# Attention backward: three one-bank buffers for the dP product, transposes in three steps, column fills of X spread singly

## The chip, the cores and the metric

The kernel runs on one core of a Trainium2 chip. The metric is the device time of one execution in microseconds (us), and the median of several executions is quoted. "PE" is the matmul engine, "PEld" its weight loads, DVE, ACT and POOL are the vector, scalar and GpSimd engines, SP issues the DMAs. A PSUM "bank" is one of eight pieces of the matmul's output memory (the Trainium skill, "PSUM — Partial Sum Buffer", Specifications (TRN2): 8 banks of 2 KiB per partition). All eight are in use in this kernel, before and after, so a bank given to one tile is taken from another.

## The reference

Forward and backward pass of an E-Branchformer block: two sequences of 4000 tokens, 144 channels, bf16. Only attention matters here:

```python
scores = jnp.einsum('btd,bsd->bts', q, k) * D ** (-0.5)
p = _softmax(scores, axis=-1)
attn = jnp.einsum('bts,bsd->btd', p, v)
# ... and the gradients of all inputs by jax.vjp with grad_out
```

The kernel folds the weights so that, for a block of 128 query rows, S = Q·xaᵀ gives the scores, dP = B·xaᵀ the gradient of the probabilities, P = exp(S), Sm = dP*P, and then y needs the transposes of P and Sm (by DMA), and the "column fills" X = Smᵀ·Qs + Pᵀ·Bt are added into an accumulator in SBUF.

## The kernel before

There are 32 rows (blocks of 128 queries) per sequence, and four units (1000 key columns each) per row. The program fixes PE's order; the other engines' orders come from the compiler's scheduler.

```python
ps_s = tile_pool(name="at_pss", bufs=1, space=PSUM)   # S: one tile of 2 banks
ps_d = tile_pool(name="at_psd", bufs=1, space=PSUM)   # dP: one tile of 2 banks
ps_x = tile_pool(name="at_psx", bufs=2, space=PSUM)   # X: 2 tiles of 1 bank
ps_y = tile_pool(name="at_psy", bufs=1, space=PSUM)   # y: 1 bank
ps_j = tile_pool(name="at_psj", bufs=1, space=PSUM)   # transposes: 1 bank

def unit(i, c2):                     # (cut)
    pS = ps_s.tile([128, 2, 512], F32, tag="S")
    pD = ps_d.tile([128, 2, 512], F32, tag="D")
    for r, (p_, h) in enumerate(((pS, 0), (pD, 0), (pS, 1), (pD, 1))):   # the four "remainder" products (16 channels)
        nc.tensor.matmul(p_[:, h, 0:SC], QBr[rr, bi, :], S.XR[rr, c2, 0:SC], start=True, stop=False)
    for p_, w_ in ((pS, QTm), (pD, BTm)):                                # 128 channels, S then dP
        for h in range(2):
            nc.tensor.matmul(p_[:, h, 0:SC], w_[:, bi, :], S.xaT[:, c0:c0 + SC], start=False, stop=True)
    nc.scalar.activation(pd, pS[:, :, 0:SC], ACT.Exp, accum_out=...)      # P
    for h in range(2):
        nc.vector.scalar_tensor_tensor(Sm[...], pD[:, h, 0:SC], 1.0, P[...], op0=ALU.mult, op1=ALU.mult, accum_out=...)

def xfill(pr, f):                    # (cut) 12 matmuls; pr: a pair of rows, f: one of 11 column groups
    X = ps_x.tile([128, 3, D], F32, tag="x")
    ...
    if f % 3 == 2:                   # emptied by ACT, added by POOL
        nc.scalar.copy(xs[:, 0:nj, :], X[:, 0:nj, :])
        nc.gpsimd.tensor_tensor(a_, xs[:, 0:nj, :], a_, op=ALU.add)
    else:                            # added by DVE straight from X
        nc.vector.tensor_tensor(a_, X[:, 0:nj, :], a_, op=ALU.add)

nfill = [1, 1, 2, 1, 1, 2, 1, 2]     # fills in the 8 units of two rows
for i in range(NBK + 2):             # (cut)
    for c2 in range(4):
        unit(i, c2)
        yz(i - 2, c2)                # 16 matmuls of y for the row before last
        if c2 == 3: row_end(i)       # l, rl, dd, nd, nr, Qs, br, Bt; starts the two DMA transposes
        if i % 4 == 2 and c2 == 1: jit(i // 4 + 1)    # 12 transposes of Q and B for the next four rows, 3 copies by DVE
        # then this unit's nfill[...] fills
```

## Time and profile before

| | before |
|---|---|
| time, median of 3 | 1789.49 us (1781.45 to 1790.64) |
| attention stretches, first to last exp | 472.8 and 470.8 us |
| four rows in the middle (median) | 58.8 us |
| of four rows, dP waiting for Sm | 3.65 us |
| of four rows, transposes waiting for their copies | 2.03 us |

How to read it. The windows view gives the busy time of each engine in a stretch. This is one from the middle of the first attention stretch (columns as its header says):

```profile
core 0: us, PE busy (x) PEld busy (x) DVE busy (x) ACT busy (x) POOL busy (x), PEclk, DMA share, GB/s
300.00:650.00 350.00, 338.16 (x3874) 245.40 (x3871) 205.93 (x657) 137.44 (x272) 60.87 (x104) 1.00 0.82 145
```

PE is busy 97% of it at full clock and no other engine comes near. But the Trainium skill warns of that number ("Perfetto Trace Analysis", Identifying the Most-Contended Engine): matmul occupancy does not measure the distance to the roof, because matmuls are pipelined. What helps is the distance between the starts of one matmul and the next. In the timeline y and X matmuls start every 0.062 us although each is listed with 0.23 us. All waits in this text are such distances, less the usual one.

The transposes, in the view of waits (engine, line, waited for whom, total us, times, longest):

```profile
engine line waited for: us in total, times, longest us
...
PE pj L1635 <- DVE QTm L1636: 6.0, 5, 1.2
...
PE pj L1635 <- DVE BTm L1636: 2.6, 5, 0.5
```

That is 300 us of the trace (350 to 650 us). The three groups of four transposes share one bank, so the second and the third wait until DVE has copied the one before. (The view leaves out what overlaps with the modelled tail of a matmul; by start distances it is 2.0 us per group of four rows.)

### The profile page before, as it was taken

Reading aid. Unit: us, or ns where it says so; the run is one execution under the profiler, and the core shown is the slowest. Engines: PE = TensorE matmul, PEld = TensorE weight load, DVE = VectorE, ACT = ScalarE, POOL = GpSimd, SP = SyncE. Lnnn points to the kernel's source line nnn. Section 1 sums busy time; section 2 is a strip of 40 time slices with the busy share of each in tenths; the row PEclk is TensorE's granted clock in tenths of the full one; section 3 lists DMA queues with packets and bytes.
Section 4 is the critical chain, followed back from the end, with each engine's and each line's share of the span. In section 5 each row is a group of like instructions: output and inputs, shape, how many; then the busy total and the mean of one; then the engine's idle time right before and its main releaser. Section 6 shows DMA issues by size and latency. Waiting matters only on the chain.

```text
span 1788.5 us, 38445 instructions
## 1 busy us (share of the span) xinstructions
PE 1398.8 (78%) x15110; PEld 1035.2 (58%) x15110; DVE 1042.9 (58%) x3693; ACT 577.9 (32%) x1275; POOL 486.0 (27%) x831
## 2 busy tenths in 40 slices
PE   6666338999999999976566644899999999986663
PEld 3455315676667667866445431567766776776641
DVE  5778954665566555312877894555565655521393
ACT  3444213343334334211244421334333333411020
POOL 2666411111111111102766641111111111110160
PEclk9777557999999999998788855899999999999775
DMA  3111216787879788544411121788877887854320
GB/s 90 47 60 35 60 31 119 142 154 135 143 142 153 143 143 153 134 122 107 122 54 60 34 61 39 132 142 150 139 143 141 154 143 139 156 116 122 97 61 10
DMA packets 614882, 193.44 MB, mean 108 GB/s; under 512 B 584132, under 2 KB 610436, under 8 KB 614692
## 3 DMA queue, kind: packets, MB, share of 16 engines
q1 hardware_dynamic: 613828, 190.81, 54.2%
q8 instruction: 120, 1.97, 0.4%
q14 instruction: 70, 0.57, 0.1%
q10 hardware_dynamic: 864, 0.09, 0.0%
HBM read 37.48 MB, written 12.06 MB: 28 GB/s over the span
## 4 chain that ended last, share of the span: by engine, by line
PE 52%; DVE 22%; issue 8%; POOL 7%; SPq 4%; ACT 3%; DMA 3%; POOLq 0%; DVEq 0%; ACTq 0%
PE y L1692 11%; PE pS L1654 8%; PE X L1711 6%; PE X L1710 6%; DVE Sm L1660 5%; PE pD L1654 5%; PE pS L1650 4%; SPq L1348 4%; PE pD L1650 3%; ACT Pm L1657 2%; POOL gn_t L1515 2%; DVE goT L1590 1%; PE po L1790 1%; POOL rstd_g L1511 1%; PE EF L1776 1%
## 5 line engine op out<-in xcount | busy, mean ns | idle before, releaser
L1660 DVE SCALAR_TENSOR_TENSOR Sm<-pD,Pm 128x500 bf16<-128x500 f32 x512 | 326.8, 675 | 349.0 <-ACT Pm L1657 349.0
L1657 ACT ACTIVATE Pm<-pS 128x1000 bf16<-128x1000 f32 x256 | 256.9, 1003 | 516.7 <-PE pS L1654 516.7
L1711 PE MATMUL X<-Bt,Pm 128*128 128x144 bf16 x2048 | 282.1, 226 | 0.5 <-DVE Bt L1680 0.5
L1710 PE MATMUL X<-Qs,Sm 128*128 128x144 bf16 x2048 | 282.2, 226 | 0.0
L1710 PEld LDWEIGHTS <-Sm 128*128 128x128 bf16 x2048 | 200.4, 98 | 0.8 <-issue 0.8
L1711 PEld LDWEIGHTS <-Pm 128*128 128x128 bf16 x2048 | 200.4, 98 | 0.0
L1650 PE MATMUL pS<-XR,QBr 16*128 16x500 bf16 x512 | 162.0, 395 | 7.0 <-ACT Pm L1657 6.0
L1654 PE MATMUL pS<-xaT,QTm 128*128 128x500 bf16 x512 | 161.6, 399 | 0.0
L1654 PE MATMUL pD<-xaT,BTm 128*128 128x500 bf16 x512 | 159.2, 394 | 0.0
L1692 PEld LDWEIGHTS <-ST 128*128 128x128 bf16 x2048 | 138.9, 99 | 28.5 <-issue 1.6
L1692 PEld LDWEIGHTS <-PT 128*128 128x128 bf16 x2048 | 138.0, 98 | 29.3 <-issue 2.2
L1692 PE MATMUL y<-xaa,ST 128*128 128x144 bf16 x2048 | 151.0, 228 | 0.0
L1692 PE MATMUL y<-xaa,PT 128*128 128x144 bf16 x2048 | 149.9, 227 | 0.7 <-DVE B_t L1700 0.5
L1716 POOL TENSOR_TENSOR acc_3148<-xs,acc_3148 128x432 f32<-128x432 f32 x48 | 52.9, 1102 | 240.6 <-ACT xs L1715 240.6
L1716 POOL TENSOR_TENSOR acc_15091<-xs,acc_15091 128x432 f32<-128x432 f32 x48 | 52.9, 1101 | 238.9 <-ACT xs L1715 238.9
L1650 PE MATMUL pD<-XR,QBr 16*128 16x500 bf16 x512 | 103.4, 391 | 16.2 <-DVE Sm L1660 12.0
L1650 PEld LDWEIGHTS <-QBr 16*128 16x128 bf16 x1024 | 40.6, 91 | 110.8 <-issue 81.4
L1677 POOL TENSOR_SCALAR Qs<-Q_t,rl 128x144 bf16<-128x144 bf16 x64 | 24.6, 384 | 256.8 <-DVE rl L1669 207.5
L1715 ACT COPY xs<-X 128x432 f32<-128x432 f32 x96 | 49.7, 518 | 132.2 <-PE X L1711 132.2
L1654 PEld LDWEIGHTS <-BTm 128*128 128x128 bf16 x512 | 52.2, 102 | 65.0 <-issue 11.1
L1718 DVE TENSOR_TENSOR acc_3148<-X,acc_3148 128x432 f32<-128x432 f32 (+1 forms) x128 | 74.1, 582 | 20.4 <-PE X L1711 20.3
L1718 DVE TENSOR_TENSOR acc_15091<-X,acc_15091 128x432 f32<-128x432 f32 (+1 forms) x128 | 74.1, 582 | 18.8 <-PE X L1711 18.7
(1282 smaller groups left out, 2727.4 us busy)
## 6 DMA issues: line engine op xcount, KB each, us to landing
gs<-in_grad_out_dram SPq DMA_DIRECT2D x24, 720.0 KB, 5.2
gs<-in_grad_out_dram SPq DMA_DIRECT2D x8, 540.0 KB, 4.0
xg<-in_x_dram SPq DMA_DIRECT2D x28, 144.0 KB, 2.4
dh_d_491<-dh SPq DMA_DIRECT2D x8, 288.0 KB, 3.0
dh<-dh_d_491 SPq DMA_DIRECT2D x8, 288.0 KB
dh_d_12434<-dh SPq DMA_DIRECT2D x8, 288.0 KB, 2.3
dh<-dh_d_12434 SPq DMA_DIRECT2D x8, 288.0 KB, 3.0
out_dram<-og SPq DMA_DIRECT2D x14, 144.0 KB, 3.8
```

Of the source, the lines that this page charges most:

```text
L1348: nc.sync.dma_start(self.r[m * DR:(m + 1) * DR, g % self.ring, :], self.st[self.p0 + DR:self.p0 + 32, g * 512 + m:g * 512 + m + w])
L1515: nc.gpsimd.tensor_scalar(gn_t[g][:, hf * 2 + q, :], h_[:, q, D:2 * D], nm[:, q:q + 1], rstd_g[:, i0 + q:i0 + q + 1], op0=ALU.add, op1=ALU ...
L1650: nc.tensor.matmul(p_[:, h, 0:SC], QBr[rr, bi, :], S.XR[rr, c2, 0:SC], start=True, stop=False)
L1654: nc.tensor.matmul(p_[:, h, 0:SC], w_[:, bi, :], S.xaT[:, c0:c0 + SC], start=False, stop=True)
L1657: nc.scalar.activation(pd, pS[:, :, 0:SC], ACT.Exp, accum_out=st["l", i][:, c2:c2 + 1])
L1660: nc.vector.scalar_tensor_tensor(Sm[:, pb, c1:c1 + SC], pD[:, h, 0:SC], 1.0, P[:, pb, c1:c1 + SC], op0=ALU.mult, op1=ALU.mult, accum_out=s ...
L1692: nc.tensor.matmul(y[:, w, :], src[:, tb, j, :], S.xaa[:, j, :], start=(j == 0), stop=(j == NBK - 1))
L1710: nc.tensor.matmul(X[:, jj, :], Sm[:, pb, j * 128:(j + 1) * 128], Qs[:, pb, :], start=(kk == 0), stop=False)
L1711: nc.tensor.matmul(X[:, jj, :], P[:, pb, j * 128:(j + 1) * 128], Bt[:, pb, :], start=False, stop=(kk == 1))
L1715: nc.scalar.copy(xs[:, 0:nj, :], X[:, 0:nj, :])
L1716: nc.gpsimd.tensor_tensor(a_, xs[:, 0:nj, :], a_, op=ALU.add)
L1718: nc.vector.tensor_tensor(a_, X[:, 0:nj, :], a_, op=ALU.add)
```

## The change

The intent is to take both waits from PE. dP gets three one-bank buffers, so its bank is free earlier; X pays with one of its two banks. To live with one X bank, the eleven fills of a pair of rows no longer stand two in a row but before and after the y products ("places"). The transposes are done in three steps in three different units, their copies go to ACT, small operations move from DVE to POOL and ACT, and exp and Sm get a raised priority in the scheduler. The diff is whole:

```diff
--- before.py
+++ after.py
@@ -1604,8 +1604,8 @@
         sm = es.enter_context(tc.tile_pool(name="at_sm", bufs=4))
         xp = es.enter_context(tc.tile_pool(name="at_xs", bufs=2))
         ps_s = es.enter_context(tc.tile_pool(name="at_pss", bufs=1, space=PSUM))
-        ps_d = es.enter_context(tc.tile_pool(name="at_psd", bufs=1, space=PSUM))
-        ps_x = es.enter_context(tc.tile_pool(name="at_psx", bufs=2, space=PSUM))
+        ps_d = es.enter_context(tc.tile_pool(name="at_psd", bufs=3, space=PSUM))
+        ps_x = es.enter_context(tc.tile_pool(name="at_psx", bufs=1, space=PSUM))
         ps_y = es.enter_context(tc.tile_pool(name="at_psy", bufs=1, space=PSUM))
         ps_j = es.enter_context(tc.tile_pool(name="at_psj", bufs=1, space=PSUM))
         P = ab.tile([128, NP, GW], BF, name="Pm")
@@ -1622,19 +1622,17 @@
         jt = {}
         id_ = W.ident
 
-        def jit(g):
+        def jit(g, step):
             r = slice(g * 4, g * 4 + 4)
-            QTm = xp.tile([128, 4, 128], BF, tag="QTm")
-            BTm = xp.tile([128, 4, 128], BF, tag="BTm")
-            QBr = xp.tile([128, 4, 128], BF, tag="QBr")
-            for off, src in ((0, S.Q_t), (32, S.B_t), (64, S.Q_t), (96, S.B_t)):
-                nc.gpsimd.tensor_scalar(QB[:, :, off:off + DR], src[:, r, 128:D], 1.0, 0.0, op0=ALU.mult, op1=ALU.add)
-            for dst, src in ((QTm, S.Q_t[:, r, 0:128]), (BTm, S.B_t[:, r, 0:128]), (QBr, QB[:])):
-                pj = ps_j.tile([128, 4, 128], BF, tag="j")
-                for j in range(4):
-                    nc.tensor.transpose(pj[:, j, :], src[:, j, :], id_[:])
-                nc.vector.tensor_copy(dst[:], pj[:])
-            jt[g] = (QTm, BTm, QBr)
+            if step == 0:
+                jt[g] = [xp.tile([128, 4, 128], BF, tag=t_, name=t_) for t_ in ("QTm", "BTm", "QBr")]
+                for off, src in ((0, S.Q_t), (32, S.B_t), (64, S.Q_t), (96, S.B_t)):
+                    nc.gpsimd.tensor_scalar(QB[:, :, off:off + DR], src[:, r, 128:D], 1.0, 0.0, op0=ALU.mult, op1=ALU.add)
+            src = (S.Q_t[:, r, 0:128], S.B_t[:, r, 0:128], QB[:])[step]
+            pj = ps_j.tile([128, 4, 128], BF, tag="j")
+            for j in range(4):
+                nc.tensor.transpose(pj[:, j, :], src[:, j, :], id_[:])
+            nc.scalar.copy(jt[g][step][:], pj[:])
 
         def unit(i, c2):
             g, bi = divmod(i, 4)
@@ -1644,21 +1642,22 @@
                 st["l", i] = sm.tile([128, 4], F32, tag="l4", name="l4")
                 st["d", i] = sm.tile([128, 8], F32, tag="d8", name="d8")
             pS = ps_s.tile([128, 2, 512], F32, tag="S")
-            pD = ps_d.tile([128, 2, 512], F32, tag="D")
-            for r, (p_, h) in enumerate(((pS, 0), (pD, 0), (pS, 1), (pD, 1))):
+            pD = [ps_d.tile([128, 512], F32, tag="D", name="pD") for h in range(2)]
+            for r, o_ in enumerate((pS[:, 0, 0:SC], pD[0][:, 0:SC], pS[:, 1, 0:SC], pD[1][:, 0:SC])):
                 rr = slice(32 * r, 32 * r + DR)
-                nc.tensor.matmul(p_[:, h, 0:SC], QBr[rr, bi, :], S.XR[rr, c2, 0:SC], start=True, stop=False)
-            for p_, w_ in ((pS, QTm), (pD, BTm)):
+                nc.tensor.matmul(o_, QBr[rr, bi, :], S.XR[rr, c2, 0:SC], start=True, stop=False)
+            c0 = 2 * c2 * SC
+            for h in range(2):
+                nc.tensor.matmul(pS[:, h, 0:SC], QTm[:, bi, :], S.xaT[:, c0 + h * SC:c0 + (h + 1) * SC], start=False, stop=True)
+            for h in range(2):
+                nc.tensor.matmul(pD[h][:, 0:SC], BTm[:, bi, :], S.xaT[:, c0 + h * SC:c0 + (h + 1) * SC], start=False, stop=True)
+            with tc.high_priority():
+                pd = P[:, pb, c0:c0 + 2 * SC].rearrange("p (h c) -> p h c", h=2)
+                nc.scalar.activation(pd, pS[:, :, 0:SC], ACT.Exp, accum_out=st["l", i][:, c2:c2 + 1])
                 for h in range(2):
-                    c0 = (2 * c2 + h) * SC
-                    nc.tensor.matmul(p_[:, h, 0:SC], w_[:, bi, :], S.xaT[:, c0:c0 + SC], start=False, stop=True)
-            c0 = 2 * c2 * SC
-            pd = P[:, pb, c0:c0 + 2 * SC].rearrange("p (h c) -> p h c", h=2)
-            nc.scalar.activation(pd, pS[:, :, 0:SC], ACT.Exp, accum_out=st["l", i][:, c2:c2 + 1])
-            for h in range(2):
-                c1 = c0 + h * SC
-                nc.vector.scalar_tensor_tensor(Sm[:, pb, c1:c1 + SC], pD[:, h, 0:SC], 1.0, P[:, pb, c1:c1 + SC], op0=ALU.mult, op1=ALU.mult,
-                                               accum_out=st["d", i][:, 2 * c2 + h:2 * c2 + h + 1])
+                    c1 = c0 + h * SC
+                    nc.vector.scalar_tensor_tensor(Sm[:, pb, c1:c1 + SC], pD[h][:, 0:SC], 1.0, P[:, pb, c1:c1 + SC], op0=ALU.mult, op1=ALU.mult,
+                                                   accum_out=st["d", i][:, 2 * c2 + h:2 * c2 + h + 1])
 
         def row_end(i):
             pb = i % NP
@@ -1670,13 +1669,13 @@
             dd = sm.tile([128, 1], F32, tag="dd")
             nc.vector.reduce_sum(dd[:], d8[:], axis=AX.X)
             nd = sm.tile([128, 1], F32, tag="nd", bufs=6)
-            nc.vector.tensor_scalar(nd[:], dd[:], rl[:], -1.0, op0=ALU.mult, op1=ALU.mult)
+            nc.gpsimd.tensor_scalar(nd[:], dd[:], rl[:], -1.0, op0=ALU.mult, op1=ALU.mult)
             nr = sm.tile([128, 1], F32, tag="nr", bufs=6)
-            nc.vector.tensor_scalar(nr[:], nd[:], rl[:], None, op0=ALU.mult)
+            nc.gpsimd.tensor_scalar(nr[:], nd[:], rl[:], 1.0, op0=ALU.mult, op1=ALU.mult)
             st["rl", i], st["nr", i] = rl, nr
             nc.gpsimd.tensor_scalar(Qs[:, pb, :], S.Q_t[:, i, :], rl[:], 1.0, op0=ALU.mult, op1=ALU.mult)
             br = sm.tile([128, D], F32, tag="br")
-            nc.gpsimd.tensor_scalar(br[:], S.B_t[:, i, :], rl[:], 1.0, op0=ALU.mult, op1=ALU.mult)
+            nc.scalar.activation(br[:], S.B_t[:, i, :], ACT.Copy, scale=rl[:])
             nc.vector.scalar_tensor_tensor(Bt[:, pb, :], Qs[:, pb, :], nd[:], br[:], op0=ALU.mult, op1=ALU.add)
             tb = i % NT
             nc.sync.dma_start_transpose(out=PT[:, tb], in_=P[:, pb, :])
@@ -1717,25 +1716,28 @@
             else:
                 nc.vector.tensor_tensor(a_, X[:, 0:nj, :], a_, op=ALU.add)
 
-        nfill = [1, 1, 2, 1, 1, 2, 1, 2]
-        jit(0)
+
+        fills = {(0, 0): 0, (1, 0): 1, (1, 1): 2, (2, 0): 3, (3, 0): 4, (4, 0): 5, (4, 1): 6, (5, 0): 7, (6, 0): 8, (7, 0): 9, (7, 1): 10}
+        jsteps = {(1, 1): 0, (2, 1): 1, (3, 0): 2}
+        for step in range(3):
+            jit(0, step)
         with tc.manual_schedule(engines={mybir.EngineType.PE}):
             for i in range(NBK + 2):
+                pr, half = i // 2 - 1, i % 2
                 for c2 in range(4):
                     if i < NBK:
                         unit(i, c2)
-                    if 0 <= i - 2 < NBK:
-                        yz(i - 2, c2)
+                    for place in range(2):
+                        f = fills.get((half * 4 + c2, place))
+                        if f is not None and 0 <= pr < NBK // 2:
+                            xfill(pr, f)
+                        if place == 0 and 0 <= i - 2 < NBK:
+                            yz(i - 2, c2)
                     if c2 == 3 and i < NBK:
                         row_end(i)
-                    if i % 4 == 2 and c2 == 1 and i // 4 + 1 < NGR:
-                        jit(i // 4 + 1)
-                    pr = i // 2 - 1
-                    if 0 <= pr < NBK // 2:
-                        s = (i % 2) * 4 + c2
-                        f0 = sum(nfill[:s])
-                        for f in range(f0, f0 + nfill[s]):
-                            xfill(pr, f)
+                    g = i // 4 + 1
+                    if (i % 4, c2) in jsteps and g < NGR:
+                        jit(g, jsteps[i % 4, c2])
 
 
 def phase_merge_out(k, W, b, S):
```

## The prediction

> **What bounds the kernel.** By the windows table the two attention stretches (about 250-720 and 1095-1570 us) take 53% of the time and there PE is busy 48 of every 50 us at a granted clock of 1.00; DVE 29.5, ACT 20. So PE is nearly the limit there and only its stalls can be won. In the timeline the exps of one row of four units start 14.2, 14.0, 14.2 and 16.3 us after the last row's; the 16.3 is the row with the transposes.
>
> Start-to-start times of the matmuls in 350-700 us give one unit: four remainder products 0.31 us, S and dP 0.86, y 16 x 0.0625 = 1.0, fills 1.0 on average (128 matmuls in 8 units), changes 0.1: 3.28 us, 26.2 for two rows. Measured are 28.2 plus 1.05 for half of a transpose group. The missing 2.0 us is the second dP remainder waiting for the second Sm multiply of the unit before: 22.6 us in 96 units, 0.235 each. The loop is closed by latency: remainder to S 0.31, to exp 0.63, to first Sm 1.22, first Sm 0.6, second 0.68, release 0.06: 3.5 us. PE keeps matmul order (the Trainium skill, "PSUM — Partial Sum Buffer", Engine vs sequencer instructions); the trace agrees: S waits behind the blocked dP remainder.
>
> **What the change does.**
> 1. Three dP banks: that remainder waits for the first Sm, so the loop is 2.9 us, under PE's 3.28. Removes up to 2.0 us per two rows. In rows 0 and 1 (4.06 us per unit at the lower clock, 1.32 us of wait) about 0.67 per unit goes: 11 us in all.
> 2. Transposes: a group costs 2.1 us now, from waits for DVE copies (0.4 us each) on one bank. Twelve transposes at 0.055 are 0.66; spread, about 0.95 with changes. Saves 1.15 x 14 = 16 us.
> 3. X falls to one bank. A DVE add is 0.60 us, an ACT copy 0.52; between two fills of one unit lies 1.0 us of y. If DVE runs the add as soon as X is done, no stall. But X is done just as the exp is (both about 2.15 us after the unit's start), and the Sm multiplies have priority: behind them the add ends 1.9 us later and the second fill waits 1.0 us. Two of three double units use DVE: up to 2.1 us per two rows, 67 us over 32 pairs, cancelling step 1.
> 4. The first fill of a pair now precedes y, so Bt is needed 1.0 us sooner; Bt was ready just as the fill began (both 507.3 us). Up to 1.5 us per pair if adds go first. nd and nr on POOL and br on ACT shorten little.
>
> **Sum.** Step 1 at most 64 us, rows 0-1 11, step 2 16: 91 us, 1698. Steps 3 and 4 take back some 20 to 75 of it. I take 53: **1752 us**, 8 in 10 in **1708 to 1786**. Faster 0.52, within 2% 0.44, slower 0.04.
>
> **What would show it.** Step 1: the wait of dP remainders for Sm nearly gone, ordinary rows 13.2-13.8 us. Step 2: the 16.3 us row becomes at most 0.9 above others, no transpose waiting for a copy. Step 3: X matmuls waiting for an acc add, 1 us, in units with two fills. Step 4: X waiting for Bt at each pair's start.
>
> **What would make it wrong.** An order on DVE or ACT that delays exp or Bt (br behind an exp) brings it near 1789; adds and Bt both in time bring 1700.

## More of the kernel before

The groups of the page that matter (line, engine, operation, output and inputs, shapes, count; busy us and mean ns; idle time of the engine before them and what ended it):

```profile
L1660 DVE SCALAR_TENSOR_TENSOR Sm<-pD,Pm 128x500 bf16<-128x500 f32 x512 | 326.8, 675 | 349.0 <-ACT Pm L1657 349.0
L1657 ACT ACTIVATE Pm<-pS 128x1000 bf16<-128x1000 f32 x256 | 256.9, 1003 | 516.7 <-PE pS L1654 516.7
...
L1710 PE MATMUL X<-Qs,Sm 128*128 128x144 bf16 x2048 | 282.2, 226 | 0.0
...
L1650 PE MATMUL pD<-XR,QBr 16*128 16x500 bf16 x512 | 103.4, 391 | 16.2 <-DVE Sm L1660 12.0
```

The last line is the only large PE group that waits for Sm. One such wait in the timeline (start, length, engine, line, operation; in brackets the idle time before):

```profile
537.76 0.67 DVE L1660 SCALAR_TENSOR_TENSOR Sm<-pD,Pm 128x500 bf16<-128x500 f32 x1
...
538.35 0.67 DVE L1660 SCALAR_TENSOR_TENSOR Sm<-pD,Pm 128x500 bf16<-128x500 f32 x1
...
538.67 0.38 PE L1650 MATMUL pS<-XR,QBr 16*128 16x500 bf16 x1
...
538.95 0.09 DVE L1660 DVE_READ_ACCUMULATOR Sm<-pD,Pm 128x1 f32 x1
539.09 0.37 PE L1650 MATMUL pD<-XR,QBr 16*128 16x500 bf16 x1
539.10 0.38 PE L1650 MATMUL pS<-XR,QBr 16*128 16x500 bf16 x1
539.10 0.38 PE L1650 MATMUL pD<-XR,QBr 16*128 16x500 bf16 x1
...
539.41 0.60 PE L1654 MATMUL pS<-xaT,QTm 128*128 128x500 bf16 x2
...
540.05 1.00 ACT L1657 ACTIVATE Pm<-pS 128x1000 bf16<-128x1000 f32 x1 [0.70 <-PE pS L1654]
```

The reader is to see that the first S remainder starts at 538.67, and the next product in PE's order, the first dP remainder, only at 539.09, just after the second Sm multiply has ended. dP is one tile of two banks, and it comes free as a whole. The S products, ready long before, stand behind it, because matmuls run in program order (the Trainium skill, "PSUM — Partial Sum Buffer", Engine vs sequencer instructions: matmuls start and complete in program order; the trace agrees here). So the wait is 0.42 us, it delays the exp too, and it happens in 9 of 16 units.

## The result, and the profile after

| | before | after |
|---|---|---|
| time, median of 4 | 1787.69 us (1781.45 to 1790.64) | 1765.88 us (1763.78 to 1767.97) |
| ratio | | 0.9883 (95% interval 0.9852 to 0.9913) |
| attention stretches, first to last exp | 472.8 and 470.8 us | 459.5 and 459.5 us |
| four rows in the middle (median) | 58.8 us | 57.7 us |

A ratio is the mean time of one kernel's fast runs over that of the other's of the same rounds, so it is not quite the ratio of the medians quoted. The kernel is 1.2% faster: clear of noise, and under 2%. Both profiled executions differ by 24.6 us (spans 1788.5 and 1763.9), and the two attention stretches by 13.3 + 11.3 = 24.6: all of it is there.

The same window after. PE does more matmuls (3964 instead of 3874) and is *less* busy:

```profile
300.00:650.00 350.00, 327.96 (x3964) 246.19 (x3962) 195.43 (x605) 158.79 (x323) 65.80 (x129) 1.00 0.83 147
```

The page's groups that answer to those of before, with X added:

```profile
L1659 DVE SCALAR_TENSOR_TENSOR Sm<-pD,Pm 128x500 bf16<-128x500 f32 x512 | 327.1, 677 | 401.2 <-ACT Pm L1656 401.2
L1656 ACT ACTIVATE Pm<-pS 128x1000 bf16<-128x1000 f32 x256 | 256.5, 1002 | 295.7 <-PE pS L1651 290.6
L1709 PE MATMUL X<-Qs,Sm 128*128 128x144 bf16 x2048 | 292.4, 226 | 58.0 <-DVE acc_15219 L1717 18.2
...
L1648 PE MATMUL pD<-XR,QBr 16*128 16x500 bf16 x512 | 112.1, 395 | 1.9
```

The wait of the dP remainders has gone from 16.2 to 1.9 us, and X, which had 0.0, now has 58.0 (the page's idle times cover the whole run and leave out what overlaps with the modelled end of a matmul). The view of waits (350 to 650 us) shows the new wait and no line any more for a transpose waiting for a copy. (The second line is the same wait for an add; it names the small `l` because that instruction follows the add on DVE.)

```profile
PE X L1709 <- DVE acc_3148 L1717: 11.9, 14, 0.9
...
PE X L1709 <- DVE l L1666: 5.1, 6, 0.9
```

One such wait in the timeline, in a unit with two fills:

```profile
511.82 1.00 ACT L1656 ACTIVATE Pm<-pS 128x1000 bf16<-128x1000 f32 x1 [1.93 <-PE pS L1651]
...
512.73 0.23 PE L1710 MATMUL X<-Bt,Pm 128*128 128x144 bf16 x1
512.79 1.16 PE L1691 MATMUL y<-xaa,PT 128*128 128x144 bf16 x16
512.95 0.68 DVE L1659 SCALAR_TENSOR_TENSOR Sm<-pD,Pm 128x500 bf16<-128x500 f32 x1 [1.22 <-ACT Pm L1656]
...
513.55 0.67 DVE L1659 SCALAR_TENSOR_TENSOR Sm<-pD,Pm 128x500 bf16<-128x500 f32 x1
514.15 0.08 DVE L1659 DVE_READ_ACCUMULATOR Sm<-pD,Pm 128x1 f32 x1
514.15 0.60 DVE L1717 TENSOR_TENSOR acc_3148<-X,acc_3148 128x432 f32<-128x432 f32 x1
514.81 0.22 PE L1709 MATMUL X<-Qs,Sm 128*128 128x144 bf16 x1 [0.85 <-DVE acc_3148 L1717]
```

The first fill ends at about 512.96 (its last matmul starts at 512.73). At that moment the exp is done too, and DVE takes the two Sm multiplies first. The add that empties X starts at 514.15, 1.2 us later. PE, which could have gone on after the 16 y matmuls at about 513.8, stands until 514.81.

So the expected gain was made and then given back at a new wait. The experiments settle how much each part is worth.

### The profile page after: what moved, and what is told of

It reads as the page before. It is cut to its first block, busy times and chain, and to the rows that moved or that the text cites. A ratio compares the mean times of both kernels' runs of the same rounds, so it can differ in the third digit from the quotient of the medians.

```text
span 1763.9 us, 38409 instructions
## 1 busy us (share of the span) xinstructions
PE 1355.7 (77%) x15110; PEld 1024.0 (58%) x15110; DVE 1001.3 (57%) x3517; ACT 624.6 (35%) x1387; POOL 494.8 (28%) x895
## 4 chain that ended last, share of the span: by engine, by line
PE 42%; DVE 25%; ACT 10%; issue 8%; POOL 6%; DMA 4%; SPq 4%; POOLq 0%; DVEq 0%; ACTq 0%
ACT Pm L1656 8%; PE y L1691 8%; PE pS L1651 7%; DVE Sm L1659 7%; PE X L1709 6%; PE X L1710 5%; PE pS L1648 4%; SPq L1348 3%; PE pD L1653 3%; POOL gn_t L1515 2%; DMA gs<-in_grad_out_dram 2%; DVE goT L1590 1%; PE EF L1778 1%; POOL rstd_g L1511 1%; PE po L1792 1%
## 5 line engine op out<-in xcount | busy, mean ns | idle before, releaser
L1709 PE MATMUL X<-Qs,Sm 128*128 128x144 bf16 x2048 | 292.4, 226 | 58.0 <-DVE acc_15219 L1717 18.2
L1710 PE MATMUL X<-Bt,Pm 128*128 128x144 bf16 x2048 | 292.6, 226 | 3.2 <-DVE Bt L1679 3.2
L1691 PEld LDWEIGHTS <-PT 128*128 128x128 bf16 x2048 | 134.4, 99 | 1.0 <-issue 1.0
L1691 PEld LDWEIGHTS <-ST 128*128 128x128 bf16 x2048 | 132.5, 98 | 0.0
L1648 PE MATMUL pD<-XR,QBr 16*128 16x500 bf16 x512 | 112.1, 395 | 1.9
L1672 POOL TENSOR_SCALAR nd<-dd,rl 128x1 f32<-128x1 f32 x64 | 17.1, 267 | 334.7 <-DVE rl L1668 334.7
L1648 PE MATMUL pS<-XR,QBr 16*128 16x500 bf16 x512 | 103.2, 396 | 6.4 <-ACT Pm L1656 5.0
L1651 PEld LDWEIGHTS <-QTm 128*128 128x128 bf16 x512 | 29.3, 98 | 71.8 <-issue 71.8
```

Of the source, the lines that this page charges most:

```text
L1648: nc.tensor.matmul(o_, QBr[rr, bi, :], S.XR[rr, c2, 0:SC], start=True, stop=False)
L1651: nc.tensor.matmul(pS[:, h, 0:SC], QTm[:, bi, :], S.xaT[:, c0 + h * SC:c0 + (h + 1) * SC], start=False, stop=True)
L1691: nc.tensor.matmul(y[:, w, :], src[:, tb, j, :], S.xaa[:, j, :], start=(j == 0), stop=(j == NBK - 1))
L1709: nc.tensor.matmul(X[:, jj, :], Sm[:, pb, j * 128:(j + 1) * 128], Qs[:, pb, :], start=(kk == 0), stop=False)
L1710: nc.tensor.matmul(X[:, jj, :], P[:, pb, j * 128:(j + 1) * 128], Bt[:, pb, :], start=False, stop=(kk == 1))
```

## The experiments

All are edits of the changed kernel except e4, which is an edit of the kernel before. Every kernel gave the right result. Each was timed in four executions (three rounds and the profiled one), on one of two chips, beside runs of the kernel before on the same chip (medians 1784.83 to 1785.03 us).

This table is worked out from the traces' start times, for rows 4 to 23 of the first sequence (the mean of five times four rows). A wait is the distance from the start of the matmul before, less the usual 0.004 (remainders), 0.056 (transposes) or 0.062 us (y, X). "Rest" is what remains of the row time.

| kernel | time, us | ratio to before | four rows | dP waits for Sm | X waits for bank | X waits for Qs, Bt | transposes wait | rest |
|---|---|---|---|---|---|---|---|---|
| before | 1785 | 1 | 59.11 | 3.65 | 0 | 0 | 2.03 | 53.4 |
| after | 1765.9 | 0.9883 | 57.71 | 0 | 4.66 | 0 | 0 | 53.05 |
| e4 before, split transposes | 1757.9 | 0.9840 | 56.76 | 3.66 | 0 | 0 | 0 | 53.1 |
| e5 after, unsplit transposes | 1804.0 | 1.0107 | 60.58 | 0 | 4.65 | 0 | 1.95 | 54.0 |
| e3 after, D two, X two banks | 1772.2 | 0.9929 | 57.88 | 2.87 | 0 | 2.03 | 0 | 53.0 |
| e6 after, no raised priority | 1763.5 | 0.9875 | 57.71 | 0 | 4.66 | 0 | 0 | 53.05 |
| e7 after, two adds earlier | 1751.0 | 0.9812 | 56.68 | 0 | 2.25 | 1.38 | 0 | 53.05 |
| e2 after, fills 1, 5, 9 by ACT | 1709.7 | 0.9584 | 53.77 | 0 | 0.61 | 0.11 | 0 | 53.05 |
| e9 e2, br on POOL | 1717.4 | 0.9618 | 54.35 | 0 | 0 | 1.29 | 0 | 53.06 |
| e1 after, X two banks (shared) | 1728.4 | 0.9678 | 55.37 | 0 | 0 | 2.04 | 0.27 | 53.06 |
| e10 e1, first fill behind y | 1700.1 | 0.9527 | 54.05 | 0.72 | 0 | 0 | 0.27 | 53.06 |
| e8 e1 and e2 together | 1694.9 | 0.9487 | 53.17 | 0 | 0 | 0.10 | 0 | 53.07 |
| e11 e8, first fill behind y | 1689.6 | 0.9463 | 53.07 | 0 | 0 | 0 | 0 | 53.07 |

The split of X's waits between "bank" and "Qs, Bt" goes by what the matmul needs and by the view of waits of each run. The rest is 53.0 to 53.1 us wherever no transposes bunch up: that is PE's own work, and everything above it is waiting. (In the kernel before and in e5 the rest also holds dips of the granted clock and waits of y; in the kernel before a row of 18.0 instead of 16.3 us is among them, in a stretch with a mean clock of 0.97.)

### e1: X gets its second bank back

There is no ninth bank, so X and the transposes share a pool of two.

```diff
-        ps_x = es.enter_context(tc.tile_pool(name="at_psx", bufs=1, space=PSUM))
+        ps_x = es.enter_context(tc.tile_pool(name="at_psx", bufs=2, space=PSUM))
-        ps_j = es.enter_context(tc.tile_pool(name="at_psj", bufs=1, space=PSUM))
...
-            pj = ps_j.tile([128, 4, 128], BF, tag="j")
+            pj = ps_x.tile([128, 4, 128], BF, tag="x", name="pj")
```

> The changed kernel with X back at two banks; the second bank is the transposes' own, which X and the transposes now share in turn (D keeps three). Theory A, the one X bank is what eats the gain: the three waits of 1.0, 0.3 and 1.0 us per two rows of the changed kernel go, four rows take 53.1 us instead of 57.7, and with 30 pairs of rows at 2.3 us the time falls by about 70 us to 1697 (1690 to 1710). Rival B, the rows are held at 14 us by something behind that wait (Bt, the DMA transposes, the DVE queue), so the wait only moves: 1745 or more, with new waits of X or y in the same units.

Measured: 1728.38 us, ratio 0.9678. The X waits for the bank went entirely (4.66 to 0 per four rows), and the rows fell by 2.3 us. That is half of what theory A promised; rival B is right for the other half. The view of waits of e1 (350 to 650 us) names the new one:

```profile
PE X L1708 <- POOL Qs L1675: 5.7, 11, 0.5
...
PE X L1709 <- DVE Bt L1678: 2.0, 11, 0.2
```

Eleven pairs of rows, eleven waits for Qs and eleven for Bt, all in the first fill of a pair: by start distances 0.68 + 0.34 us. They had been hidden in the changed kernel, because there PE lost 1.0 us at the last double unit of a pair, just before.

### e2: the same one bank, emptied by ACT

```diff
-            if f % 3 == 2:
+            if f in (1, 5, 9):
                 xs = xp.tile([128, 3, D], F32, tag="xs")
```

> The changed kernel, still one X bank, but the first fill of each double unit (1, 5, 9 instead of 2, 5, 8) leaves X by the ACT copy, not by the DVE add that stands behind both Sm multiplies. Theory A: waits of 1.0 us become 0.3, as in the one double unit that ACT already serves; 1.4 us less per two rows, about 43 us less, 1723 (1712 to 1735). If instead the bank itself needs more time than the 1.0 us of y whoever empties it, the three waits stay at 1.0 and the time at 1766.

Measured: 1709.74 us, ratio 0.9584. With one X bank still, two of the three waits went to 0 and the third stayed at 0.30 us: better than expected, because I had taken 0.3 us for all three. So one bank is enough if the right engine empties it; a second bank, as in e1, removes the wait as well. What decides with one bank is who empties it: DVE, behind 1.2 us of Sm multiplies, or ACT, which has just finished the exp. A unit of e2 with two fills in the timeline:

```profile
519.40 1.16 PE L1691 MATMUL y<-xaa,ST 128*128 128x144 bf16 x16
519.56 0.68 DVE L1659 SCALAR_TENSOR_TENSOR Sm<-pD,Pm 128x500 bf16<-128x500 f32 x1 [1.22 <-ACT Pm L1656]
519.66 0.52 ACT L1714 COPY xs<-X 128x432 f32<-128x432 f32 x1
520.40 0.23 PE L1709 MATMUL X<-Qs,Sm 128*128 128x144 bf16 x1
```

The copy starts 0.1 us after the first Sm multiply, next to it, and the second fill starts 1.00 us after the first y matmul: 16 times 0.0625, so without a wait. Nor is Qs late here (0.11 us in four rows). The likely reason is that without the add of fill 9 the row's end gets through DVE sooner.

### e3: the bank trade undone

```diff
-        ps_d = es.enter_context(tc.tile_pool(name="at_psd", bufs=3, space=PSUM))
-        ps_x = es.enter_context(tc.tile_pool(name="at_psx", bufs=1, space=PSUM))
+        ps_d = es.enter_context(tc.tile_pool(name="at_psd", bufs=2, space=PSUM))
+        ps_x = es.enter_context(tc.tile_pool(name="at_psx", bufs=2, space=PSUM))
```

> The changed kernel with the bank given back: D two one-bank buffers, X two. Fill places, split transposes and moved small operations stay. Theory A, the two halves of the bank trade are about equal: waits of X go (4.7 us per four rows), waits of the second dP remainder for the second Sm multiply come back, about 0.45 us in each of ten units of sixteen (4.5 us); 1750 to 1770, so the same as the changed kernel. Rival, the third D bank is what made the change faster: 1780 or more.

Measured: 1772.22 us, ratio 0.9929, four rows 57.88 against 57.71. As expected the trade is nearly even, but with other terms: dP's waits came back with 2.87 us, not 4.5, and 2.03 us of waits for Qs and Bt came with them, as in e1. In e3 dP is two tiles of one bank each, so its halves come free separately. The first dP remainder then waits in none of the 80 units, but the second waits for the second Sm multiply in 40 of them. So, as far as e3 shows, cutting the tile in two is worth only 0.8 of the 3.65 us; with the third bank the rest goes too.

### e4: only the transposes split

The three-step `jit` of the change, called as the change calls it, put into the kernel before; the copies stay on DVE, banks and fills stay as they were. (The diff is cut: the body of `jit` and its first call, split in the same way, are left out.)

```diff
+        jsteps = {(1, 1): 0, (2, 1): 1, (3, 0): 2}
...
-                    if i % 4 == 2 and c2 == 1 and i // 4 + 1 < NGR:
-                        jit(i // 4 + 1)
+                    g = i // 4 + 1
+                    if (i % 4, c2) in jsteps and g < NGR:
+                        jit(g, jsteps[i % 4, c2])
```

> The kernel before with only the transposes split into three steps (copies still on DVE). Theory A, the 22 us that the change gained are the transposes' gain, with the bank trade near zero: 2.0 us less in every fourth row, 14 groups, 28 us: 1760 (1752 to 1770), every row 14.0 to 14.6. Rival, splitting only matters together with the D banks: 1780 or more.

Measured: 1757.94 us, ratio 0.9840. This one part gives 27 us, more than the whole change's 22. By the rows (56.76 against 57.71 us) the kernel before with split transposes is ahead of the changed kernel in the middle of the stretch; in whole times the two intervals (0.9812 to 0.9867 and 0.9852 to 0.9913) overlap a little, and they were not run in the same rounds, so I claim only that the split alone gives as much as the whole change. Since its copies stay on DVE, their move to ACT is not needed for that.

### e5: the change without the split

```diff
-                    if (i % 4, c2) in jsteps and g < NGR:
-                        jit(g, jsteps[i % 4, c2])
+                    if (i % 4, c2) == (2, 1) and g < NGR:
+                        for step in range(3):
+                            jit(g, step)
```

> The changed kernel with the transposes unsplit: all twelve in one unit of every fourth row, their copies on ACT. Theory A: splitting is worth the same 2 us per four rows here as in the kernel before (27 us by e4), so 1793 (1785 to 1802), and D and X banks alone make the kernel no faster than before. Rival: the copies on ACT or the X waits already hide it, 1775 or less.

Measured: 1803.96 us, ratio 1.0107: slower than before, and 38 us slower than the changed kernel. Together with e4: the split is worth 27 us in the kernel before and 38 us here; the banks, fills and moved operations without it lose 19 us.

### e6: no raised priority

```diff
-            with tc.high_priority():
+            if True:
```

> The changed kernel without the raised priority of exp and Sm multiplies. By the instruction order only the first rows of each batch differ: in steady rows the adds stand behind both Sm multiplies anyway, because the multiplies come first in the program. Theory: the X waits of 1.0 us are there as before and the time is 1766 within 0.4%. Rival (my prediction's words, the multiplies stand first because of their priority): the adds move in front and the time falls by 20 us or more.

Measured: 1763.45 us, ratio 0.9875 (the changed kernel 0.9883). The waits are to the hundredth the same. In the two traces DVE's order of instructions in attention differs only in the first rows of each sequence (Bt moves in front of a second Sm multiply), and ACT's and POOL's not at all. The Sm multiplies stand in front of the add without help: they come first in the program.

### e7: two of the adds moved forward

```diff
+            elif f in (1, 9):
+                with tc.high_priority():
+                    nc.vector.tensor_tensor(a_, X[:, 0:nj, :], a_, op=ALU.add)
             else:
                 nc.vector.tensor_tensor(a_, X[:, 0:nj, :], a_, op=ALU.add)
```

> The changed kernel with the adds of fills 1 and 9 raised in the DVE order: by the instruction order they now stand between the two Sm multiplies of their unit instead of behind both. One X bank, everything else as changed. Theory (the bank is freed late because of its place in the DVE queue, not because an add is too slow): X is free 0.6 us earlier, the wait falls from 1.0 to 0.4 us in two of the three double units, 1.2 us per two rows, 36 us: 1730 (1720 to 1742). Rival: the delayed second Sm multiply makes the dP products wait instead: 1755 or more.

Measured: 1750.97 us, ratio 0.9812. X's wait in these units fell from 1.01 to 0.41 us, exactly as expected, and dP did not wait (0). The time fell by 15 us and not by 36, because the wait for Qs and Bt came up from under it: 0.69 us at each pair's first fill. So moving one instruction up DVE's queue by one place shortens the wait by 0.6 us, the length of one Sm multiply: the wait is the queue.

### e9: br back to POOL

```diff
# on top of e2
-            nc.scalar.activation(br[:], S.B_t[:, i, :], ACT.Copy, scale=rl[:])
+            nc.gpsimd.tensor_scalar(br[:], S.B_t[:, i, :], rl[:], 1.0, op0=ALU.mult, op1=ALU.mult)
```

> e2 with the br product back on POOL, where it was in the kernel before. Theory: the one wait of 0.3 us that e2 keeps (second fill of the fifth unit of a pair) comes from br on ACT standing in front of that unit's exp and delaying the copy of X; it goes, 0.6 us per four rows, 9 us, if Bt is not late again: 1701 (1694 to 1708). Rival: POOL does nd, Qs, nr and br one after the other and Bt comes 0.4 us later, so the first fill of a pair waits for it: 1710 or more.

Measured: 1717.41 us, ratio 0.9618, slower than e2's 0.9584. Both theories were right at once. The wait of 0.3 us went (br on ACT does stand in front of that exp), and Bt came late by 0.65 us per pair. So on top of e2 the place of br on ACT is worth 8 us.

### e10, e8, e11: towards the sum of PE's work

```diff
# e10: on top of e1.   e11: on top of e8 (= e1 and e2)
-        fills = {(0, 0): 0, (1, 0): 1, ...
+        fills = {(0, 1): 0, (1, 0): 1, ...
```

> e1 (X two banks, shared with the transposes) came out at 1728, not 1697; its trace shows new waits of X for Bt of about 0.7 and 0.3 us in the first unit of every pair of rows. Here only the first fill of a pair moves back behind y, where the kernel before had it. Theory: Bt is late because the fill was moved 1.0 us forward in front of it; then these waits go, four rows fall from 55.4 to about 53.3 and the time to 1698 (1690 to 1706). Rival: the wait follows the DVE's backlog (adds in front of the row's end) and stays in part wherever the fill is: 1710 or more.

Measured e10: 1700.10 us, ratio 0.9527. The waits for Qs and Bt are gone, so the place of the fill was the cause; 0.36 us of dP waiting came back in the unit after. In e11, where ACT and not DVE empties that unit's first fill, it is not there, so DVE's queue is the likely cause.

> e1 and e2 together: X two banks shared with the transposes, and the first fills of the double units leave by ACT, which takes an add of fill 9 off the DVE queue in front of Bt. Theory: X waits go as in e1, and Bt is not late as in e2, so four rows fall to about 53.1 us, the sum of PE's own work: 1700 (1694 to 1707). Rival: once X never waits, Bt is late whichever engine empties fill 9: 1715 or more, with waits of X for Bt in the first unit of a pair.

Measured e8: 1694.90 us, ratio 0.9487, four rows 53.17 us.

> e8 with the first fill of a pair behind y as well (as e10). In steady rows it should add nothing to e8 if Bt is already in time; at the first pair of each batch, where the first fill of the changed kernel waits 1.9 us for Bt at the low clock, it saves about 3 us a batch: 1694 (1686 to 1702). If e10's wait of 0.36 us of the dP remainder in the second unit comes back, 0.7 us per four rows, it is no faster than e8.

Measured e11: 1689.58 us (1688.42 to 1692.52), ratio 0.9463 (0.9444 to 0.9482): 5.4% faster than before and the best version found. The two attention stretches are 3.3 and 3.4 us shorter than in e8, about the 3 us expected at the first pair. It has no wait on PE in any steady row, and no dP wait like e10's. The windows view of e11 for the same stretch:

```profile
300.00:650.00 350.00, 350.00 (x4303) 266.01 (x4301) 215.11 (x665) 170.89 (x351) 71.32 (x141) 1.00 0.91 159
```

4303 matmuls instead of 3874 in 350 us. What is left in the steady rows is PE's own work. The DMA share has risen from 0.82 to 0.91, so the transposes by DMA may be the next limit; no run here shows it.

## Why the prediction was right or wrong

The time, 1765.9 us, lies in the range 1708 to 1786; the central value was 14 us too low. "Within 2%" had 0.44 and "faster" 0.52, so the class forecast leaned to the wrong side.

- **What bounds the kernel: right.** PE's work of two rows was put at 26.2 us by start distances. All kernels without bunched transposes show 53.0 to 53.1 us for four rows once the waits are taken off, 26.5 for two, with the 0.67 us of transposes per four rows in it; e11 runs at that.
- **Step 1, three dP banks: mechanism right, size nearly.** Predicted up to 2.0 us per two rows; 1.83 went (3.65 per four). One detail was misread: it is the first dP remainder that waits, because dP was one tile of two banks and came free as a whole. (With the tile cut in two, in e3, it is the second, as predicted.)
- **Rows 0 and 1: right, but in part given back.** The unit fell from 4.05 to 3.42 us, 5.1 us per sequence (predicted: 11 in all). But the first unit of row 2, from remainder to remainder, then took 8.11 instead of 6.13 us (8.11 instead of 5.80 in the second sequence). Its first fill stands before y, and Bt is made after two more Sm multiplies and a late br:

```profile
274.39 0.33 PE L1709 MATMUL X<-Qs,Sm 128*128 128x144 bf16 x1
...
274.56 0.40 ACT L1678 ACTIVATE br<-B_t,rl 128x144 f32<-128x144 bf16 x1
...
275.89 0.37 DVE L1679 SCALAR_TENSOR_TENSOR Bt<-Qs,nd,br 128x144 bf16<-128x144 bf16 x1
276.31 0.28 PE L1710 MATMUL X<-Bt,Pm 128*128 128x144 bf16 x1 [1.59 <-DVE Bt L1679]
```

  The y matmuls of the first two units of row 2 start 0.120 us apart instead of 0.062; the granted clock there is 0.50. The Trainium skill, "TensorE: Matmul & The Clock Gate", What's actually happening, says that the clock is at half rate after idleness. The trace of the changed kernel agrees for the time before attention (clock 0.50 from 212 to 244 us, with PE busy at most 0.6 of every 4 us). But the clock then stayed at 0.50 until about 280 us, through rows 0 and 1, in which PE was busy 3.4 to 3.5 of every 4 us. So idleness alone does not explain the low clock of these rows; why it stayed is open.
- **Step 2, the split: right in kind, the most mis-sized term.** Predicted 16 us; e4 measured 27 in the kernel before and e5 38 in the changed one. I charged the split group 0.95 us. Its twelve transposes cost 0.67 us in the changed kernel, and in e4 the group adds less still to four rows (56.76 against 56.54 us for the last four rows of a sequence, which have none), presumably because part of it fits into the waits for dP. I had also left out what follows a bunched group, dips of the clock and waits of y (the "rest" of e5 is 0.9 us longer).
- **Step 3, one X bank: right, and at its worst case.** The case "Sm first" came true: 1.01 us in the two double units that DVE empties. The third, emptied by ACT, waits 0.30 us, which I had put at nothing: br on ACT delays the exp and the copy there. Together 2.33 us per two rows against "up to 2.1". Over 30 pairs of rows that is 70 us. I had taken 53 us for steps 3 and 4 together, a middle between two cases that exclude each other. That choice is the step that failed in the sum. It is also why ordinary rows did not fall to the predicted 13.2 to 13.8 us: they take 14.1 to 14.8.
- **The reason given for step 3, "the Sm multiplies have priority": wrong.** e6 shows that the raised priority changes nothing in steady rows; program order does it.
- **Step 4, Bt for the first fill: hidden.** No steady row of the changed kernel waits for Bt; the stall of X just before gives it time. e1 and e7 bring it out as soon as X waits less (1.02 and 0.69 us per pair), and e10 shows its cause.
- **"nd and nr on POOL and br on ACT shorten little": wrong for br.** By e9, on top of e2, br on ACT is worth 0.65 us of Bt's wait per pair. nd itself got no shorter: 0.267 us on POOL, 0.21 on DVE.

Put together for the time: dP's waits give 3.65 x 15 = 55 us, the split 27, the first rows about 6 (10 less 4 given back); X's waits take 4.66 x 15 = 70 (15 groups of four rows in both sequences have fills). That makes 18 us, against 22 measured. So more than the whole dP gain was lost again at X, and what is left of the change is part of the split's. e8, in which the X waits are gone, is 71 us faster than the changed kernel, which agrees with the 70. That the central value came within 14 us is partly luck: the split was put 11 us too low, while the dP gain was put 9, the first rows 5 and the loss at X 17 us too favourably.

Left open: how much each move of the small operations to POOL (nd, nr) is worth by itself was not tried, nor were the places of the fills other than a pair's first, nor the copies of the transposes put back on DVE in the changed kernel.

## What to carry to other kernels

When all PSUM banks are taken, a bank given to one product can be a wait given to another, as here, where the trade was nearly even (e3); before such a trade, look at which engine empties the poorer tile and what stands before it in that engine's queue at that moment. Here two waits of 1.0 us went without any bank, by letting the engine that is free just then empty the three fills that matter. After removing a wait, look for the one that it hid (here Qs and Bt): only the sum of PE's start distances, 53.05 us for four rows, told when there was none left.

## What the Trainium skill lacked or had wrong

- "Perfetto Trace Analysis", Optimization Strategy, says that consistent bubbles can mean there isn't enough SBUF or PSUM for the next tile. The bubble of 1.01 us here can be read so, and a second bank does remove it (e1: 4.66 to 0 us per four rows). That passage does not name the other reading, the queue of the emptying engine: e2 removed most of it with the same one bank (4.66 to 0.61). The page's way, to look for what blocks, names the add in both readings; the start of the emptying instruction (514.15, 1.2 us after its input was done) points to the queue.
- The same page, Matmuls, advises to rotate independent groups through different banks. It does not say what a tile of two banks costs: the first dP remainder waited 0.4 us for the second half of a tile of which the first half was free. Two tiles of one bank (e3) removed that wait, but 2.87 of 3.65 us per four rows remained at the second remainder.
- "GPSIMD Engine Reference", Elementwise — side-by-side cycle accounting, compares large operations (2048 elements). For the smallest one (128x1, nd) this case shows 0.267 us on POOL against 0.21 us on DVE, as the profile lists them (POOL's listed spans are rough), so the gap there is small.
- What the skill says of the busy share of matmuls held: 338 of 350 us before, 328 after with more matmuls done.
